# Splitting weights on the side: first parts in two small tiles, second parts in place, and output weights loaded two by two

## The chip, the core and the metric

The kernel runs on one core of a Trainium2 chip, in one launch. Engines named here: TensorE (PE in the profile; PEld is its weight load), VectorE (DVE), ScalarE (ACT), GpSimd (POOL), and SyncE (SP, which here only issues DMAs). The metric is the device time of one launch in microseconds, median of several runs. The kernel before takes 1472.05 us (three runs, 1471.54 to 1473.36).

## The reference

Eight batches of eight attention heads (sequence 576, head dimension 64) go through a landmark attention; the result, 4608 tokens of 512, through two expert layers:

```python
A, Bm, C = sm(q, k_lm), sm(q_lm, k_lm), sm(q_lm, k)      # 32 landmarks
for _ in range(6):
    Z = 2 * Z - Z @ Bm @ Z
x = A @ Z @ C @ v                    # then reshaped to (4608, 512)
x = ((x @ w1) * (x @ w2) @ w3) @ w_out            # d_ff 1024
h = x @ w_in                                      # d_ff 2048
out = where(h > 0, h, exp(min(h, 0)) - 1) @ w_out
```

The weights arrive as float64.

## The kernel before

Matrix products are done in a split form: a float32 value is cut into a first part (`hi`, rounded to the form in which TensorE multiplies) and a second part (`lo`, what is left), and a product takes three matmuls (hi by hi, hi by lo, lo by hi).

Three stages follow each other. In the first, some 117 us, the weights of the first layer are converted from float64 and `w3 @ w_out` is formed. In the second, up to some 690 us, the eight batches run: attention of the next batch, made of small matmuls and many small steps on DVE and ACT, is woven into the matmuls of the first layer (lines 689 to 691, `ab`, and 716 to 718, `y`). A batch has 16 units, a unit has two half steps, and after each half step `fill` (line 874) issues what stands in the tables: steps of the attention of the next batch, loads of `k` (unit 6), `v` (11) and `q` (14) for the batch after the next, and one tick of a `Pipe`. In the third, 690 us to the end, the second layer runs: 72 steps `hh(u)` (42 matmuls, 7 products of half-size blocks, lines 794 to 796, tile `hm`) and `oo(u)` (24 matmuls, lines 849 to 851, tile `o`), two steps apart. `hh(u)` needs the weights `wh` of its step, loaded again for each step into three buffers (`load_wh`, line 738); `oo(u)` needs two of the 16 tiles `wo2`, loaded once (`load_wo`, line 743).

What the change touches is the preparation of these weights in the second stage. `pipe2` holds 32 jobs as Python generators: for each of 8 pairs `p`, two jobs (`wh_first`, `wh_second`) that turn 256 rows of `w_in` into a float32 tile `wx` of seven blocks, and two (`wo_job`) that make a tile of `w_out`. A `yield` ends a job's part of a half step. `join_bits` (line 148) loads the float64 values (SP, line 154), waits two half steps, takes an absolute value on ACT (line 162), four steps on DVE (169 to 172), and two on POOL (174, 176). Then `spill_parts` (line 180) makes both parts on POOL (a cast, line 185, and a subtraction, line 186) in one tile `hl`, and writes it to DRAM by a DMA on SP (line 189): four times for a `wx`, once for a tile of `w_out`. The tile `hl` is there once; a mutex (`hold("hl")`) lets one such piece be under way at a time in program order, and the next cast waits on the chip until the write has read the tile.

Each engine works through its own instructions in the order in which the program issues them, and SP's DMA instructions wait in line too: a load behind a write isn't issued before the write is. POOL also makes the second part `atl` of the attention matrix (line 513), which the matmuls of line 690 need, and issues all loads of `wh` and `wo2` in the third stage.

```python
hl = mlp.tile([128, 2, 512], F32R, name=nm, tag="w2c")
pool.tensor_copy(hl[:, 0, :n], x)
pool.tensor_tensor(hl[:, 1, :n], x, hl[:, 0, :n].bitcast(F32), op=ALU.subtract)
for _ in range(GAP):
    yield
sp.dma_start(out=dst, in_=hl[:, :, :n].bitcast(F32))
held.remove("hl")
```

Of the kernel before, what the change touches and what calls it, by code (L numbers as in the profile page):

```python
# [8 lines left out]
F32 = mybir.dt.float32  # L9
F32R = mybir.dt.float32r  # L10
# [4 lines left out]
ALU = mybir.AluOpType  # L15
# [13 lines left out]
K2 = F2 // 128  # L29
# [7 lines left out]
NPAIR = K2 // 2  # L37
# [9 lines left out]
KS = 15  # L47
QS = 20
RATE = 1.6
GAP = 1  # L50
CONV = (1, 5, 11, 14, 18)
M2 = 5
M3 = 10
# [11 lines left out]
def nystrom_moe_kernel(ctx, tc, qT, kT, vm, vr, w12, w3T, w_out1, w_in2, w_out2, out):  # L65
    nc = tc.nc
    pe, dve, act, pool, sp = nc.tensor, nc.vector, nc.scalar, nc.gpsimd, nc.sync
# [69 lines left out]
            if c.done is not None:  # L137
                c.done()

    held = set()  # L140

    def hold(what):

        while what in held:
            yield
        held.add(what)

    def join_bits(c, ahead=2, ready=lambda: True):

        n = 512
        c.raw = c.p.tile([128, 4 * n + 4], U16, name=f"{c.nm}_raw", tag="raw", bufs=3)
        sp.dma_start(out=c.raw[:, 1 : 1 + 4 * n], in_=c.src.bitcast(U16))
        c.top = c.raw[:, 4 : 4 + 4 * n : 4]
        c.mid = c.raw.bitcast(U32)[:, 1 : 1 + 2 * n : 2]
        for _ in range(ahead):
            yield
        while not ready():
            yield  # L160
        c.y = c.t("y", "cy", BF16)
        act.activation(c.y, c.top.bitcast(BF16), AF.Abs)
        yield
        yield from hold("join")
        c.two, c.tt = c.t("s", "cs", U16, 1), c.t("t", "ct", F32)
        c.lead = c.t("p", "cp", U16)
        act.mul(c.tt, c.mid, 2.0 ** -36)
        yb = c.y.bitcast(U16)
        dve.tensor_scalar(yb, yb, E_MIN, E_MAX, op0=ALU.max, op1=ALU.min)
        dve.tensor_scalar(c.lead, yb, E_MIN, 8.0, op0=ALU.subtract, op1=ALU.mult)  # L170
        dve.scalar_tensor_tensor(c.lead, c.top, 0x8000, c.lead, op0=ALU.bitwise_and, op1=ALU.bitwise_or)
        dve.tensor_scalar(c.two, c.lead, 0xFF80, None, op0=ALU.bitwise_and)
        yield
        pool.tensor_tensor(c.tt, c.tt, c.two.bitcast(BF16), op=ALU.mult)
        c.x = c.x()
        pool.tensor_tensor(c.x, c.tt, c.lead.bitcast(BF16), op=ALU.add)
        held.remove("join")
        yield

    def spill_parts(nm, x, dst):  # L180

        n = x.shape[-1]
        yield from hold("hl")
        hl = mlp.tile([128, 2, 512], F32R, name=nm, tag="w2c")
        pool.tensor_copy(hl[:, 0, :n], x)
        pool.tensor_tensor(hl[:, 1, :n], x, hl[:, 0, :n].bitcast(F32), op=ALU.subtract)
        for _ in range(GAP):
            yield
        sp.dma_start(out=dst, in_=hl[:, :, :n].bitcast(F32))
        held.remove("hl")  # L190

    def wo_job(c, dst):
        yield from join_bits(c)
        yield from spill_parts(f"{c.nm}_hl", c.x, dst)

    wx = {}

# [14 lines left out]
    def wh_second(c, p):  # L212


        c.x = lambda: wx[p][:, 2:4, :].rearrange("p a n -> p (a n)")
        yield from join_bits(c, ready=lambda: p in wx)
        x = wx[p]
        a11, a12, a22, a21, s1, s2, s3 = [x[:, k, :] for k in range(7)]
        pool.tensor_tensor(s1, a21, a22, op=ALU.add)
        pool.tensor_tensor(s3, a11, a21, op=ALU.subtract)  # L220
        yield
        pool.tensor_tensor(s2, s1, a11, op=ALU.subtract)
        pool.tensor_tensor(a21, a12, s2, op=ALU.subtract)
        for k in range(0, 7, 2):
            m = min(2, 7 - k)
            yield
            yield from spill_parts(
                f"wh{p}{k}", x[:, k : k + m, :].rearrange("p a n -> p (a n)"),
                wh_d[p][:, :, k : k + m, :].rearrange("p h a n -> p h (a n)"),
            )  # L230
        held.remove("wx")

    cst = ctx.enter_context(tc.tile_pool(name="cst", bufs=1))
# [6 lines left out]
    wh_d = dram.tile([NPAIR, 128, 2, 7, 2 * 128], F32, name="wh_d")  # L240
# [324 lines left out]
    with tc.manual_schedule():  # L565
# [55 lines left out]
        for o in ORDER:  # L621
            if o == "A":
                k, n_wo = n_wo, n_wo + 1
# [49 lines left out]
        mlp = mlp_ctx.enter_context(tc.tile_pool(name="mlp", bufs=1))  # L673
# [53 lines left out]
        for p in range(NPAIR):  # L727
            pipe2.add(wh_first(Conv(cvp, f"w2{2 * p}", w_in2[2 * p]), p))
            pipe2.add(wh_second(Conv(cvp, f"w2{2 * p + 1}", w_in2[2 * p + 1]), p))
            for f in (2 * p, 2 * p + 1):  # L730
                c = Conv(cvp, f"wo2{f}", w_out2[f * 128 : (f + 1) * 128, :])
                c.x = lambda c=c: c.t("x", "cx", F32)
                pipe2.add(wo_job(c, wo_d[f]))
# [4 lines left out]
        def load_wh(u):  # L738
            t = p2r.tile([128, 2, 7, 256], F32R, name=f"wh{u}", tag="wh", bufs=NWH)
            pool.dma_start(out=t, in_=wh_d[u % NPAIR])  # L740
            wh[u] = t

        def load_wo(p, f):
            t = p.tile([128, 2, DM], F32R, name=f"wo2_{f}")
            pool.dma_start(out=t, in_=wo_d[f])
            wo2[f] = t

        def load_y(i):
            ys[i] = p2r.tile([128, KD, TB], F32, name=f"yin{i}", tag="yin")
            sp.dma_start(out=ys[i], in_=yd[:, :, i * TB : (i + 1) * TB])  # L750
# [4 lines left out]
        def sums_y(i, k):  # L755

            if k == 0:
                tv[i] = [p2r.tile([128, 2, TH], F32, name=f"tv{i}{n}", tag=f"tv{n}") for n in range(4)]
            t1, t2, t3, t4 = tv[i]
            o, a, b = (  # L760
                (t1, block(i, 0, 1), block(i, 0, 0)), (t2, block(i, 1, 1), t1),
                (t3, block(i, 1, 1), block(i, 0, 1)), (t4, block(i, 1, 0), t2),
            )[k]
            pool.tensor_tensor(o, a, b, op=ALU.subtract)

        def parts_y(i, k):

            t1, t2, t3, t4 = tv[i]
            src = (block(i, 0, 0), t2, block(i, 1, 0), t1, t3, block(i, 1, 1), t4)[k]
            hi, lo = [p2r.tile([128, 2, TH], F32R, name=f"yb{w}{i}{k}", tag=f"yb{w}{k}") for w in range(2)]  # L770
            act.copy(hi, src)
            dve.tensor_tensor(lo, src, hi.bitcast(F32), op=ALU.subtract)
            yb[i, k] = (hi, lo)
# [6 lines left out]
        def hh(u):  # L780

            i, _ = units2[u]
            w = wh.pop(u)
            ps = [ps_at.tile([128, 512], F32, name=f"hm{u}", tag="at")]
            ps += [ps_mm.tile([128, 512], F32, name=f"hm{u}{n}", tag="mm") for n in range(2)]
            ps += [ps_at.tile([128, 512], F32, name=f"hm{u}3", tag="at")]
            for k in range(7):
                bank, col = divmod(k + 1, 2)
                o = ps[bank][:, col * TH : (col + 1) * TH]
                bh, bl = yb[i, k]  # L790
                for kk in range(2):
                    cs = slice(kk * 128, (kk + 1) * 128)
                    ah, al = w[:, 0, A_OF[k], cs], w[:, 1, A_OF[k], cs]
                    pe.matmul(o, ah, bh[:, kk, :], start=(kk == 0), stop=False)  # L794
                    pe.matmul(o, ah, bl[:, kk, :], start=False, stop=False)  # L795
                    pe.matmul(o, al, bh[:, kk, :], start=False, stop=(kk == 1))  # L796
            hq[u] = ps
# [6 lines left out]
        def first(u):  # L804
            sq[u] = p2r.tile([128, 1, TH], F32, name=f"s1{u}", tag="s1", bufs=2)
            act.copy(sq[u][:, 0, :], hq[u][0][:, TH:])
# [86 lines left out]
        for u in range(nu + LAG):  # L893
            if u < nu:
                b, n, fc = units[u]
# [34 lines left out]
        p2 = ctx.enter_context(tc.tile_pool(name="p2", bufs=1))  # L930
# [6 lines left out]
        for f in range(4):  # L937
            load_wo(p2, f)
        load_wh(NWH)
        for f in range(4, K2):  # L940
            load_wo(p2, f)
        for u in range(1, n2 + LAG2):
            if u < n2:
                i, p = units2[u]
                if u > 1 and u + NWH - 1 < n2:
                    load_wh(u + NWH - 1)
                hh(u)
                first(u)
                if i + 1 < NBL:
                    if p == 1:  # L950
                        load_y(i + 1)
                    if 3 <= p < 7:
                        sums_y(i + 1, p - 3)
                    if p == NPAIR - 1:
                        for k in range(7):
                            parts_y(i + 1, k)
                combine(u)
                elu(u)
            if u >= LAG2:
                oo(u - LAG2)  # L960
# [51 lines left out]
```

## Time and profile before

| | |
|---|---|
| median of the runs | 1472.05 us |
| the profiled execution | 1470.82 us |
| its span | 1469.0 us |
| PE busy | 1383.8 us (94%) |
| DVE busy | 1084.8 us (74%) |
| ACT busy | 630.7 us (43%) |
| POOL busy | 368.2 us (25%) |
| mean granted TensorE clock | 0.979 of full |

A busy PE is not PE at its peak, and where the granted clock is below 1.00 a matmul takes longer, so time is lost in busy stretches as well. A view of waits says which engine sat idle before which line, and what released it. A release by several semaphores is put down to the one that came last.

### The profile page before, as it was taken

What the parts mean: (1) busy time and instruction counts of PE and PEld (TensorE: products, weight loads), DVE (VectorE), ACT (ScalarE), POOL (GpSimd) and SP (SyncE); (2) the same over time, 40 slices, a digit from 0 to 9 for tenths busy, and PEclk for the clock granted to TensorE, in tenths of its full rate; (3) what the DMA queues carried; (4) which work ended last, traced back from release to release, by engine and by line L of the source; (5) the groups of instructions that cost most, each with busy time, mean ns of one, the idle gap of its engine ahead of it and who ended that gap; (6) DMA issues with size and microseconds to landing.
All of it is one profiled execution on the core that took longest, in us unless ns stands there. A gap on an engine that the chain in (4) does not pass through costs nothing.

```text
span 1469.0 us, 27075 instructions
## 1 busy us (share of the span) xinstructions
PE 1383.8 (94%) x10848; PEld 1187.3 (81%) x10848; DVE 1084.8 (74%) x2003; ACT 630.7 (43%) x1266; POOL 368.2 (25%) x378
## 2 busy tenths in 40 slices
PE   5777999989899998999799999999999999999998
PEld 2335888778778786899789898989898989898987
DVE  7898778668777675653867787878788787877774
ACT  5535443434344444333434444444345353444442
POOL 4442345353545352520310201011010101101000
PEclk9988999999999999999999999999999999999999
DMA  8644243433544434241965556564655555565540
GB/s 305 227 140 147 100 167 138 153 121 128 189 142 162 153 120 157 98 174 51 378 239 202 202 192 217 192 214 166 228 181 212 196 212 197 180 229 179 187 165 29
DMA packets 56653, 259.69 MB, mean 177 GB/s; under 512 B 4816, under 2 KB 15056, under 8 KB 44240
## 3 DMA queue, kind: packets, MB, share of 16 engines
q0 software_dynamic: 12672, 140.51, 26.5%
q1 hardware_dynamic: 43856, 117.45, 22.7%
q8 instruction: 85, 1.39, 0.4%
q14 instruction: 40, 0.33, 0.1%
HBM read 216.01 MB, written 41.94 MB: 176 GB/s over the span
## 4 chain that ended last, share of the span: by engine, by line
PE 73%; DVE 11%; DMA 8%; POOL 4%; issue 2%; ACT 1%; SPq 0%; DVEq 0%; POOLq 0%; ACTq 0%
PE o L851 9%; PE o L850 9%; PE o L849 9%; PE hm L794 8%; PE hm L795 8%; PE hm L796 8%; PE y L716 3%; PE ab L689 3%; PE ab L690 3%; PE ab L691 3%; PE y L717 3%; PE y L718 3%; DMA wh_d<-wh 3%; DMA q<-in_qT_dram 2%; PE m L311 2%
## 5 line engine op out<-in xcount | busy, mean ns | idle before, releaser
L794 PE MATMUL hm<-yb,wh 128*128 128x256 f32 x1008 | 287.4, 285 | 9.9 <-DMA wh<-wh_d 6.3
L795 PE MATMUL hm<-yb,wh 128*128 128x256 f32 x1008 | 286.9, 285 | 0.0
L796 PE MATMUL hm<-yb,wh 128*128 128x256 f32 x1008 | 286.6, 284 | 0.0
L851 PE MATMUL o<-wo,el 128*128 128x512 f32 x576 | 225.6, 392 | 0.0
L850 PE MATMUL o<-wo,eh 128*128 128x512 f32 x576 | 225.3, 391 | 0.0
L849 PE MATMUL o<-wo,eh 128*128 128x512 f32 x576 | 224.0, 389 | 0.0
L825 ACT ACTIVATE t<-m 128x512 f32<-128x512 f32 x144 | 89.9, 624 | 307.0 <-DVE m L823 307.0
L794 PEld LDWEIGHTS hm<-yb,wh 128*128 128x128 f32 x1008 | 194.9, 193 | 13.6 <-issue 6.7
L795 PEld LDWEIGHTS hm<-yb,wh 128*128 128x128 f32 x1008 | 194.8, 193 | 2.8
L796 PEld LDWEIGHTS hm<-yb,wh 128*128 128x128 f32 x1008 | 194.9, 193 | 0.0
L740 POOL DMA_DIRECT2D wh<-wh_d x72 | 39.5, 549 | 616.1 <-PE hm L796 615.8
L716 PE MATMUL y<-gh,w3oh 128*128 128x288 f32 x512 | 161.5, 315 | 2.9 <-DVE w3ol L71 2.9
L689 PE MATMUL ab<-ath,mh 128*128 128x288 f32 x512 | 158.2, 309 | 5.9 <-ACT a L698 3.2
L690 PE MATMUL ab<-atl,mh 128*128 128x288 f32 x512 | 153.2, 299 | 7.2 <-POOL atl L513 7.2
L828 DVE SCALAR_TENSOR_TENSOR t<-m,t 128x512 f32<-128x512 f32 x144 | 99.0, 688 | 78.0 <-ACT m L826 78.0
L691 PE MATMUL ab<-ath,ml 128*128 128x288 f32 x512 | 152.5, 298 | 0.0
L718 PE MATMUL y<-gh,w3ol 128*128 128x288 f32 x512 | 151.7, 296 | 0.0
L717 PE MATMUL y<-gl,w3oh 128*128 128x288 f32 x512 | 151.6, 296 | 0.0
L700 DVE TENSOR_TENSOR g<-ab,a 128x288 f32<-128x288 f32 x128 | 57.7, 451 | 102.0 <-ACT gh L70 52.9
L716 PEld LDWEIGHTS y<-gh,w3oh 128*128 128x128 f32 x512 | 96.8, 189 | 42.3 <-issue 28.9
L851 PEld LDWEIGHTS o<-wo,el 128*128 128x128 f32 x576 | 108.1, 188 | 22.7
L849 PEld LDWEIGHTS o<-wo,eh 128*128 128x128 f32 x576 | 108.5, 188 | 20.9
(146 smaller groups left out, 2786.3 us busy)
## 6 DMA issues: line engine op xcount, KB each, us to landing
wh<-wh_d POOLq DMA_DIRECT2D x72, 1792.0 KB, 7.8
wo_raw<-in_w_out_dram SPq DMA_DIRECT2D x24, 512.0 KB, 5.2
wh_d<-wh SPq DMA_DIRECT2D x24, 512.0 KB, 3.3
k<-in_kT_dram SPq DMA_DIRECT2D x8, 1152.0 KB, 7.2
q<-in_qT_dram SPq DMA_DIRECT2D x8, 1152.0 KB, 6.0
yd<-ysb SPq DMA_DIRECT2D x16, 576.0 KB, 3.6
yin<-yd SPq DMA_DIRECT2D x9, 1024.0 KB, 9.9
out_dram<-osb SPq DMA_DIRECT2D x36, 256.0 KB, 2.3
```

What stands on the lines that cost most here:

```text
L689: pe.matmul(p[:, :NH], mh[:, cs], ah[:, blk, :], start=(blk == 0), stop=False)
L690: pe.matmul(p[:, :NH], mh[:, cs], al[:, blk, :], start=False, stop=False)
L691: pe.matmul(p[:, :NH], ml[:, cs], ah[:, blk, :], start=False, stop=(blk == 1))
L716: pe.matmul(a[oc][:, :NH], w3o_hi[fc][:, os_], gh, start=(fc == 0), stop=False)
L717: pe.matmul(a[oc][:, :NH], w3o_hi[fc][:, os_], gl, start=False, stop=False)
L718: pe.matmul(a[oc][:, :NH], w3o_lo[fc][:, os_], gh, start=False, stop=(fc == K1 - 1))
L794: pe.matmul(o, ah, bh[:, kk, :], start=(kk == 0), stop=False)
L795: pe.matmul(o, ah, bl[:, kk, :], start=False, stop=False)
L796: pe.matmul(o, al, bh[:, kk, :], start=False, stop=(kk == 1))
L849: pe.matmul(a, eh[:, ts_], w[:, 0, :], start=first, stop=False)
L850: pe.matmul(a, eh[:, ts_], w[:, 1, :], start=False, stop=False)
L851: pe.matmul(a, el[:, ts_], w[:, 0, :], start=False, stop=last)
```

## The change

`spill_parts` becomes `first_part`. Only the first part has a tile of its own, of half the size and in two buffers; the second part is written over the float32 values that it is made from (`wx`, or the tile `x` of `w_out`). Two pieces may be under way at a time (`spills`). A first part is written out two half steps after POOL's instructions are issued (`GAP = 2`), and the piece counts as done one half step later. Second parts are written by one DMA per `wx` (all seven blocks) and one per tile of `w_out`; `wx` is free for the next pair one half step after its write is issued. In the third stage four of the output weights' tiles are loaded ahead, and the others two by two in the steps u = 1 to 6, each time ahead of the load of `wh`.

```diff
-GAP = 1
+GAP = 2
...
-    held = set()
+    held, spills = set(), []
...
-    def spill_parts(nm, x, dst):
+    def first_part(nm, x, dst):
 
         n = x.shape[-1]
-        yield from hold("hl")
-        hl = mlp.tile([128, 2, 512], F32R, name=nm, tag="w2c")
-        pool.tensor_copy(hl[:, 0, :n], x)
-        pool.tensor_tensor(hl[:, 1, :n], x, hl[:, 0, :n].bitcast(F32), op=ALU.subtract)
+        while len(spills) > 1:
+            yield
+        spills.append(nm)
+        hi = mlp.tile([128, 512], F32R, name=nm, tag="w2c", bufs=2)
+        pool.tensor_copy(hi[:, :n], x)
+        pool.tensor_tensor(x.bitcast(F32R), x, hi[:, :n].bitcast(F32), op=ALU.subtract)
         for _ in range(GAP):
             yield
-        sp.dma_start(out=dst, in_=hl[:, :, :n].bitcast(F32))
-        held.remove("hl")
+        sp.dma_start(out=dst, in_=hi[:, :n].bitcast(F32))
+        yield
+        spills.remove(nm)
 
     def wo_job(c, dst):
         yield from join_bits(c)
-        yield from spill_parts(f"{c.nm}_hl", c.x, dst)
+        yield from first_part(f"{c.nm}_hi", c.x, dst[:, 0, :])
+        sp.dma_start(out=dst[:, 1, :], in_=c.x)
...
-            yield from spill_parts(
+            yield from first_part(
                 f"wh{p}{k}", x[:, k : k + m, :].rearrange("p a n -> p (a n)"),
-                wh_d[p][:, :, k : k + m, :].rearrange("p h a n -> p h (a n)"),
+                wh_d[p][:, 0, k : k + m, :].rearrange("p a n -> p (a n)"),
             )
+        sp.dma_start(out=wh_d[p][:, 1, :, :], in_=x)
+        yield
         held.remove("wx")
...
-        for f in range(4, K2):
-            load_wo(p2, f)
         for u in range(1, n2 + LAG2):
             if u < n2:
                 i, p = units2[u]
+                if u < NPAIR - 1:
+                    for f in (2 * u + 2, 2 * u + 3):
+                        load_wo(p2, f)
                 if u > 1 and u + NWH - 1 < n2:
                     load_wh(u + NWH - 1)
                 hh(u)
```

Three places in the order of the instructions. First POOL, in the second stage, where the blocks of the second pair (`wx1`; its pieces are `wh12` to `wh16`) and a tile of `w_out` (`wo23`) are cut up, ahead of the second part of the next attention matrix (`atl20`). Before:

```order
L174 TENSOR_TENSOR wo23_t_2694<-wo23_t_2694,wo23_s_2693 128x512
L176 TENSOR_TENSOR wo23_x_2740<-wo23_t_2694,wo23_p_2695 128x512
L185 CAST wh14_2758<-wx1_2250 128x512
L186 TENSOR_TENSOR wh14_2758<-wx1_2250,wh14_2758 128x512
L185 CAST wo23_hl_2785<-wo23_x_2740 128x512
L186 TENSOR_TENSOR wo23_hl_2785<-wo23_x_2740,wo23_hl_2785 128x512
L185 CAST wh16_2861<-wx1_2250 128x256
L186 TENSOR_TENSOR wh16_2861<-wx1_2250,wh16_2861 128x256
L513 TENSOR_TENSOR atl20_2877<-atf_2_2846,ath20_2876 128x576
```

And now:

```order
L174 TENSOR_TENSOR wo23_t_2694<-wo23_t_2694,wo23_s_2693 128x512
L176 TENSOR_TENSOR wo23_x_2743<-wo23_t_2694,wo23_p_2695 128x512
L187 CAST wo23_hi_2761<-wo23_x_2743 128x512
L188 TENSOR_TENSOR wo23_x_2743<-wo23_x_2743,wo23_hi_2761 128x512
L187 CAST wh14_2861<-wx1_2253 128x512
L188 TENSOR_TENSOR wx1_2253<-wx1_2253,wh14_2861 128x512
L519 TENSOR_TENSOR atl20_2878<-atf_2_2846,ath20_2877 128x576
L187 CAST wh16_2966<-wx1_2253 128x256
L188 TENSOR_TENSOR wx1_2253<-wx1_2253,wh16_2966 128x256
```

The subtraction now writes where it reads, and `atl20` stands ahead of the pair's last piece. Second SP, the same place in the program, with the loads of `v3`, `q3` and the next float64 weights (`w24_raw`) among the writes. Before:

```order
L189 DMA wh_d_70<-wh12_2690 256x1x512
L261 DMA v3_2742<-in_vm_dram 128x2048
L262 DMA v3_2742<-in_vr_dram 64x512
L189 DMA wh_d_70<-wh14_2758 256x1x512
L189 DMA wo_d_71<-wo23_hl_2785 128x1024
L189 DMA wh_d_70<-wh16_2861 256x1x256
L265 DMA q3_2922<-in_qT_dram 128x2304
L154 DMA w24_raw_3035<-in_w_in2_dram 128x2048
```

And now:

```order
L191 DMA wh_d_70<-wh12_2738 128x512
L191 DMA wo_d_71<-wo23_hi_2761 128x512
L198 DMA wo_d_71<-wo23_x_2743 128x512
L191 DMA wh_d_70<-wh14_2861 128x512
L271 DMA q3_2923<-in_qT_dram 128x2304
L191 DMA wh_d_70<-wh16_2966 128x256
L235 DMA wh_d_70<-wx1_2253 128x1792
L154 DMA w24_raw_3041<-in_w_in2_dram 128x2048
```

The load of `q3` stands ahead of the write of `wh16`, and the write of all second parts (`wx1`) behind it. Third POOL at the start of the third stage, (`wh3` to `wh7` are the weights of steps 3 to 7; the `tv` make block sums of `y` for the next 512 tokens). Before, from the load of the twelfth output weight on:

```order
L745 DMA wo2_11_8945<-wo_d_71 128x1024
L745 DMA wo2_12_8947<-wo_d_71 128x1024
L745 DMA wo2_13_8949<-wo_d_71 128x1024
L745 DMA wo2_14_8951<-wo_d_71 128x1024
L745 DMA wo2_15_8953<-wo_d_71 128x1024
L740 DMA wh4_9032<-wh_d_70 128x3584
L740 DMA wh5_9137<-wh_d_70 128x3584
```

And now:

```order
L746 DMA wh3_8953<-wh_d_70 128x3584
L751 DMA wo2_4_8955<-wo_d_71 128x1024
L751 DMA wo2_5_8957<-wo_d_71 128x1024
L751 DMA wo2_6_9036<-wo_d_71 128x1024
L751 DMA wo2_7_9038<-wo_d_71 128x1024
L746 DMA wh4_9040<-wh_d_70 128x3584
L751 DMA wo2_8_9145<-wo_d_71 128x1024
L751 DMA wo2_9_9147<-wo_d_71 128x1024
L746 DMA wh5_9149<-wh_d_70 128x3584
```

Before, `wo2_4` to `wo2_15` all stood between `wh3` and `wh4`; now four of them do, and two between `wh4` and `wh5`.

## Rows read from the trace of the kernel before

**Rows 1.** Windows: length, busy time by engine, granted clock, DMA share, GB/s.

```profile
160.00:690.00 530.00, 503.21 (x5291) 433.10 (x5290) 368.63 (x816) 224.99 (x539) 220.81 (x213) 0.98 0.40 141
690.00:746.00 56.00, 46.07 (x292) 42.85 (x292) 33.20 (x54) 17.67 (x33) 14.56 (x24) 0.91 0.84 311
746.00:1469.00 723.00, 719.23 (x4488) 650.73 (x4486) 554.62 (x886) 311.28 (x549) 73.52 (x94) 1.00 0.53 189
```

**Rows 2.** Timeline of PE: start, length, what, in brackets idle time and releaser.

```profile
201.10 1.69 PE L311 MATMUL m<-w_sb,z 64*32 64x512 f32 x16 [1.53 <-DVE ml L473]
573.19 1.68 PE L311 MATMUL m<-w_sb,z 64*32 64x512 f32 x16 [1.21 <-DVE ml L473]
736.69 0.55 PE L794 MATMUL hm<-yb,wh 128*128 128x256 f32 x1 [6.32 <-DMA wh<-wh_d]
```

**Rows 3.** Timeline of POOL, start of the third stage.

```profile
703.07 2.16 POOL L745 DMA_DIRECT2D wo<-wo_d  x4 [43.86 <-ACT t L825]
...
723.84 0.53 POOL L740 DMA_DIRECT2D wh<-wh_d  x1 [0.98 <-PE hm L796]
```

**Rows 4.** DMA issues: what, queue, count, KB each, median us to landing.

```profile
wh<-wh_d POOLq DMA_DIRECT2D x72, 1792.0 KB, 7.8
wh_d<-wh SPq DMA_DIRECT2D x24, 512.0 KB, 3.3
q<-in_qT_dram SPq DMA_DIRECT2D x8, 1152.0 KB, 6.0
...
wh_d<-wh SPq DMA_DIRECT2D x8, 256.0 KB, 2.7
```

**Rows 5.** Windows behind three stalls, and the one from 703 to 736.

```profile
267.00:275.00 8.00, 7.81 (x52) 5.60 (x53) 3.81 (x7) 2.81 (x7) 0.01 (x1) 0.79 0.66 241
...
563.00:570.00 7.00, 6.14 (x38) 4.35 (x39) 0.82 (x2) 1.81 (x4) 0.81 (x1) 0.62 0.85 277
...
736.00:745.00 9.00, 8.31 (x45) 8.21 (x46) 2.29 (x4) 0.37 (x1) 0.22 (x1) 0.64 0.81 324
...
703.00:736.00 33.00, 24.53 (x145) 21.82 (x144) 26.61 (x42) 14.73 (x26) 13.37 (x22) 0.94 1.11 412
```

**Rows 6.** Waits of PE from 160 to 690 us: total, times, longest.

```profile
PE ab L690 <- POOL atl L513: 7.2, 2, 4.3
PE m L311 <- DVE ml L473: 6.3, 4, 1.9
...
PE ab L689 <- ACT a L698: 3.2, 1, 3.2
PE ab L689 <- DVE g L700: 2.7, 1, 2.7
```

**Rows 7.** Chain of waits ahead of two of these stalls: start, length, what.

```profile
264.94 0.73 POOL wh L186
...
266.29 5.59 DMA q<-in_qT_dram
...
316.45 1.60 POOL wo_hl L186
...
318.51 5.52 DMA w_raw<-in_w_in_dram
```

**Rows 8.** Waits of POOL, DVE and SP's queue, whole span.

```profile
POOL wo_hl L185 <- DMA wh_d<-wh: 38.3, 12, 5.2
...
POOL wh L185 <- DMA wo_d<-wo_hl: 23.4, 9, 3.7
POOL wh L185 <- DMA wh_d<-wh: 22.9, 9, 3.5
...
DVE qsum L296 <- DMA q<-in_qT_dram: 9.3, 5, 2.5
```

**Rows 9.** The longest waits of SP's queue.

```profile
SPq L189 <- POOL wh L186: 163.0, 30, 17.4
...
SPq L189 <- POOL wo_hl L186: 90.3, 16, 8.0
```

## The prediction

> **What bounds the kernel now.** I read the windows by stage first, then who PE waits for, then the chain of waits ahead of those stalls. From 746 us on PE is busy all the time at a granted clock of 1.00 [rows 1]; nothing that the change does there can show. The first stage has the same instructions as before. What is left is 160 to 690 us, where PE is idle for 530 − 503.2 = 26.8 us and the mean clock is 0.98, and 690 to 746 us, where it is idle for 9.9 us at 0.91 [rows 1].
>
> In the second stage four kinds of wait are to be seen: for `atl` from POOL (7.2 us, two times), for `ml` from DVE (6.3, four times), for `a` from ACT (3.2) and for `g` from DVE (2.7) [rows 6], together 19.4 us. The chain shows one source behind them. POOL ends a piece of the splitting at 264.94 + 0.73 = 265.67, SP issues its write, and only then, at 266.29, the load of `q` that stood behind it; POOL at 316.45 + 1.60 = 318.05 lets go of a write, and the float64 weights behind it leave at 318.51 and land at 324.03 [rows 7]. DVE then sits at its `q` sums (9.3 us, five times [rows 8]), and ACT at its absolute value, each with work for PE behind it in its queue. POOL is late because each cast waits until the one tile `hl` has been written out: 38.3 + 23.4 + 22.9 = 84.6 us over 30 waits [rows 8]. SP's queue waits 163.0 + 90.3 = 253.3 us over 46 writes, 5.5 us each [rows 9].
>
> A stall of some 2 us or more is followed by the lower of TensorE's two clocks (1.2 in place of 2.4 GHz) for a while: over the 8 us from 267 the granted clock is 0.79, which costs 8 × 0.21 = 1.7 us; the stalls for `a`, for `g` and the longest for `ml` show the same 1.7. After the longest for `atl` it is 0.62 over 7 us [rows 5], 2.7 us, some 2.2 when the idle time in that window is left out. That makes 4 × 1.7 + 2.2 = 9.0 us. In the third stage step 4 (`hm`) starts at 736.69 after 6.32 us of waiting for its weights [rows 2], and the 9 us from 736 run at 0.64 [rows 5]: 3.2 us, some 3.0 without the idle part.
>
> **The change part by part.**
>
> *Output weights two by two.* The load of the weights for step 4 is issued at 723.84, behind 12 loads of `wo2` [rows 3], and lands when PE has waited from 730.4 on. In the window 703 to 736 the DMAs move 412 GB/s [rows 5], so bytes decide. Now eight tiles (4.2 MB) and `wh3` (1.8 MB) stand ahead of it, with its own 1.8 MB 7.9 MB in all (the size of `wh` from [rows 4]; a tile of `wo2` is 128 x 1024 float32); from 703.07 [rows 3] at 412 GB/s that lands at 703.1 + 19.1 = 722.2 by estimate, 8 us ahead of 730.4. Step 5 comes one step later (723 us [rows 1] over 68 steps of 66 matmuls, 10.6 us), and two more tiles and its weights, 2.9 MB, take 7.0 us. From then on the same 2.9 MB fall on 10.6 us, 273 GB/s, well under 412. The loads of `wo2` now wait behind a load of `wh` that waits for a buffer; the tiles of step u + 2 are asked for in step u, and used in `oo` two steps later or more. So the wait goes and its clock with it: 6.3 + 3.0 = 9.3 us. Bounds: 6.3 if the slow clock came anyway, 9.3 if not. I take 9.3, because nothing else stands still there.
>
> *Two tiles for first parts.* The 84.6 us of POOL's waits become short ones: a buffer comes round after two pieces, and the next piece is let in one half step after the write was issued. A half step is (573.19 − 201.10) / 5 / 32 = 2.3 us (the same instruction five batches apart [rows 2]), a write of 256 KB lands in 2.7 [rows 4]. So POOL waits at most some 0.4 us behind SP. Together with `atl` moving ahead of the pair's last piece this lets `atl` run earlier by the waits of the four or so pieces in a row ahead of it, 84.6 / 30 = 2.8 us each, some 11 us where 4.3 were missing.
>
> *Writes two half steps later.* SP comes to each write 2.3 us later, and POOL is done 84.6 / 46 = 1.8 us earlier on average, more at the end of a row of pieces, where `q` stands. Of 5.5 us per write 4.1 go on average. The loads behind need little: `q` was missed by 9.3 / 5 = 1.9 us [rows 8], the float64 weights by 3.2 [rows 6]. I take both as covered.
>
> *Second parts in place.* The same number of POOL instructions of the same shapes; the trace shows no subtraction that writes over its input. From nothing to twice the 0.73 us of the nearest row [rows 7], 35 us over 48 pieces, it would stay in POOL's idle time, since POOL is busy for 221 of 530 us [rows 1]; I take nothing. There are 24 more writes, 0.6 us of SP each by the 265.67 to 266.29 of [rows 7], 15 us of a queue that waited 253.
>
> *An added wait.* The next pair's first write to `wx` (POOL, line 176) now waits for the 896 KB write. Queued behind it is POOL's splitting, `atl` at times, and PE waits for that. By interpolation between 3.3 us for 512 KB and 6.0 for 1152 KB [rows 4] it lands in 4.9 us; a pair comes to that instruction no sooner than three half steps after the issue, 7.0 us. Cost between nothing and 7 times 4.9 = 34 us of POOL; I take nothing.
>
> **Sum.** 19.4 + 9.0 + 9.3 = 37.7 us if all goes and nothing comes. Other waits of PE (26.8 − 19.4 = 7.4 us) stay. Jobs shift by some half steps against the attention's steps, so ACT and DVE meet them in other places: one load of `k` now stands behind more pieces than before. I give 5 us back for new stalls, two of the size of those above with their clock. 1470.8 (the profiled execution, 1.8 of it outside the span) − 32.7 = 1438.1; the median of the runs is 1.2 above that execution: **1439 us**.
>
> **Rivals.**
>
> *SP stays the bound.* 4.1 of 5.5 us is an average; if SP still blocks `q` and the float64 weights, the change doesn't do what its delay says. Then the two stalls for `atl` go with their clock (7.2 + 1.7 + 2.2 = 11.1) and the 9.3: 1472 − 20 = 1452. For it: single waits of SP reach 17.4 us [rows 9]. Against: those long ones end with POOL's work, not with a write.
>
> *Only the third stage.* New stalls of the moved jobs eat the second stage's gain: 1472 − 9 = 1463. Against: DVE waits at five of the six loads of `q` in this stage, and where it doesn't, no stall for `ml` follows.
>
> *POOL bound by its writes: slower.* If POOL waits out every write (48 first parts at 2.7 us = 130, and 34 for `wx`: 164 us in place of 84.6), then by today's ratio of 28.4 us lost on PE for 84.6 waited the second stage loses 55 in place of 28.4; less 9.3, the time is 1472 + 17 = 1489. It decides from some 112 us of POOL waiting on, where 28.4 + 9.3 us are used up. Against it is the half step between issue and reuse. The Trainium skill has a rule in this direction ("DMA: Bandwidth & Descriptors", Anatomy of one DMA): a transfer costs about 2.0 us fixed plus its bytes at 436 GB/s, so many small ones pay more. The trace agrees on the price (by the rule 2.6 and 3.2 us, 2.7 and 3.3 measured); by the rule the 24 added writes would cost 24 × 2.0 = 48 us if each stood in the path.
>
> **How the numbers follow.** Forecast 0.65, SP stays the bound 0.16, only the third stage 0.10, slower 0.05, and 0.04 for no change in sum. The range goes from 1430, which is the full 37.7 us and some 4 of the other 7.4 us of waits, to 1462, which takes in the second case and most of the third. A measurement of this kernel can tell about 0.2%, 3 us, from no change: faster 0.91, same 0.04, slower 0.05.
>
> **What would show it.** Right: step 4 without a wait for `wh`, the clock at 1.00 from 735 on; POOL's waits for `wh_d` and `wo_d` under 20 us; no wait of DVE at `q`; PE idle in the second stage under 12 us. Wrong: waits for `atl` or `ml` still there; POOL waiting at line 176 for `wx`; SP's writes still waiting for POOL some 5 us each.

## The result and the profile after

The changed kernel takes 1436.34 us (four runs, 1435.87 to 1437.29) beside 1471.8 us before: a ratio of 0.976 with a 95% interval of 0.9743 to 0.9777, 35.5 us or 2.4% faster. The forecast was 1439. The profiled execution has a span of 1434.4 us at a mean clock of 0.989.

The windows by stage answer to [rows 1]. After the time range and its length stand the busy times of PE, PEld, DVE, ACT and POOL, then the granted clock, the DMA share and GB/s:

```profile
160.00:660.00 500.00, 487.79 (x5252) 422.87 (x5253) 370.86 (x811) 223.03 (x533) 220.91 (x213) 1.00 0.43 149
660.00:690.00 30.00, 26.39 (x202) 25.45 (x201) 15.26 (x28) 11.24 (x23) 6.40 (x12) 1.00 0.51 183
690.00:746.00 56.00, 56.00 (x347) 50.51 (x346) 47.09 (x76) 25.36 (x45) 11.55 (x16) 1.00 0.88 331
```

In the second stage PE was idle for 26.8 of 530 us; now it is for 12.2 of 500, and the mean clock is 1.00 to two places, where it was 0.98. The third stage begins with step 0, whose first matmul is in the timeline of PE, before and after:

```profile
690.09 0.28 PE L794 MATMUL hm<-yb,wh 128*128 128x256 f32 x1
```

```profile
665.63 0.28 PE L800 MATMUL hm<-yb,wh 128*128 128x256 f32 x1
```

So of the 34.6 us by which the span fell, 24.5 lie ahead of the third stage, and the rest in it: 1469.0 − 690.1 = 778.9 us before, 1434.4 − 665.6 = 768.8 after, 10.1 us.

PE's waits in the second stage, in answer to [rows 6] (total, times, longest):

```profile
PE n L418 <- DVE X L408: 4.5, 4, 1.7
PE m L317 <- DVE at L488: 3.4, 3, 2.2
PE ct L429 <- ACT e L338: 2.8, 3, 1.3
PE ab L695 <- ACT a L704: 0.9, 1, 0.9
PE m L317 <- DVE ml L479: 0.7, 1, 0.7
```

None is left for `atl` and for `g`; those for `a` and `ml` fell from 9.5 to 1.6 us. Two others grew: for `at` from 0.7 to 3.4 us, for `e` from 0.9 to 2.8. POOL waits for a write once in the whole span, in answer to [rows 8], and no line has DVE waiting for `q`:

```profile
POOL wh L187 <- DMA wh_d<-wh: 1.3, 1, 1.3
```

But SP's queue still stands at these writes, in answer to [rows 9]:

```profile
SPq L191 <- POOL wh L187: 108.9, 22, 16.1
...
SPq L191 <- POOL wo_hi L187: 55.7, 16, 6.3
```

That is 164.6 us over 38 writes, 4.3 us each, and yet the loads behind them come in time.

At the start of the third stage POOL's timeline, in answer to [rows 3], shows the weights of step 4 issued 684.57 − 678.65 = 5.9 us behind the first `wo2`, where it was 20.8 before:

```profile
678.65 2.16 POOL L751 DMA_DIRECT2D wo<-wo_d  x4 [43.77 <-ACT t L831]
680.78 0.56 POOL L746 DMA_DIRECT2D wh<-wh_d  x1
681.30 2.16 POOL L751 DMA_DIRECT2D wo<-wo_d  x4
684.57 0.53 POOL L746 DMA_DIRECT2D wh<-wh_d  x1 [1.11 <-DMA wo<-wo_d]
```

### The profile page after: what moved, and what is told of

Its sections match the earlier page's. It is cut to its first block, busy times and chain, and to the rows that moved or that the text cites. A ratio compares the mean times of both kernels' runs of the same rounds, so it can differ in the third digit from the quotient of the medians.

```text
span 1434.4 us, 27127 instructions
## 1 busy us (share of the span) xinstructions
PE 1370.2 (96%) x10848; PEld 1179.0 (82%) x10848; DVE 1088.0 (76%) x2003; ACT 630.8 (44%) x1266; POOL 368.3 (26%) x378
## 4 chain that ended last, share of the span: by engine, by line
PE 83%; DVE 13%; ACT 1%; issue 1%; DMA 1%; SPq 0%; DVEq 0%; ACTq 0%
PE o L857 9%; PE o L856 9%; PE o L855 9%; PE hm L800 8%; PE hm L801 8%; PE hm L802 8%; PE y L722 5%; PE ab L695 4%; PE ab L696 4%; PE ab L697 4%; PE y L724 4%; PE y L723 4%; PE m L317 2%; DVE w_b L128 1%; DVE w_b L124 1%
## 5 line engine op out<-in xcount | busy, mean ns | idle before, releaser
L800 PEld LDWEIGHTS hm<-yb,wh 128*128 128x128 f32 x1008 | 192.9, 191 | 6.9 <-ACT s L812 4.0
L801 PEld LDWEIGHTS hm<-yb,wh 128*128 128x128 f32 x1008 | 192.9, 191 | 2.8
L802 PEld LDWEIGHTS hm<-yb,wh 128*128 128x128 f32 x1008 | 193.0, 192 | 0.0
L855 PEld LDWEIGHTS o<-wo,eh 128*128 128x128 f32 x576 | 108.5, 188 | 20.9
L856 PEld LDWEIGHTS o<-wo,eh 128*128 128x128 f32 x576 | 108.1, 188 | 21.2
```

The lines of the kernel that those rows point to most:

```text
L855: pe.matmul(a, eh[:, ts_], w[:, 0, :], start=first, stop=False)
L856: pe.matmul(a, eh[:, ts_], w[:, 1, :], start=False, stop=False)
```

## The experiments

Ten kernels, timed against the kernel before, which measured 1471.0 to 1471.9 us in their rounds; each ratio is to the kernel before of the same round. "Second stage ends" is the start of step 0 in the profiled execution, "third" the rest of the span.

| kernel | median us | ratio, 95% | second stage ends | third |
|---|---|---|---|---|
| before | 1471.8 | | 690.1 | 778.9 |
| changed | 1436.3 | 0.9743 to 0.9777 | 665.6 | 768.8 |
| e1_gap2 | 1448.3 | 0.9822 to 0.9855 | 669.4 | 777.9 |
| e2_loads | 1464.0 | 0.9935 to 0.9964 | 691.8 | 770.8 |
| e3_all_gap1 | 1436.6 | 0.9749 to 0.9777 | 666.3 | 770.0 |
| e4_all_early | 1446.2 | 0.9814 to 0.9843 | 665.2 | 778.8 |
| f1_two_tiles_same_order | 1432.0 | 0.9706 to 0.9740 | 661.2 | 768.5 |
| f2_one_tile_same_order | 1433.4 | 0.9714 to 0.9744 | 662.6 | 769.9 |
| g1_spaced | 1445.1 | 0.9801 to 0.9834 | 664.0 | 779.6 |
| h1_early_s | 1434.8 | 0.9730 to 0.9760 | 666.6 | 767.7 |
| j1_slow_casts | 1459.7 | 0.9894 to 0.9947 | 688.6 | 770.0 |
| i1_combined | 1427.8 | 0.9674 to 0.9722 | 659.7 | 766.3 |

**The parts.** First the delay alone (on the kernel before), the loads alone (on the kernel before), and each taken out of the changed kernel.

```diff
-GAP = 1
+GAP = 2
```

> Kernel before, only GAP = 2 (writes issued two half steps after POOL's work; one tile hl with both parts). Theory A, POOL's waits on the one tile are the source: they stay at some 85 us, the two stalls for atl stay, only part of the q and float64 loads come earlier; 1462 to 1472 us. Theory B, SP's line is the source: DVE's waits at q and the stalls for a and g go with their clock (6.3 + 3.2 + 2.7 + 6.8 = 19 us), 1453 us.

1448.3 us: theory B's direction, by more than it said. What B didn't foresee is how. POOL's waits on its one tile are all still there, 39.6 + 24.0 + 17.3 + 9.1 = 90.0 us by the view of POOL's waits of this kernel:

```profile
POOL wh L185 <- DMA wh_d<-wh: 39.6, 10, 6.8
POOL wh L185 <- DMA wo_d<-wo_hl: 24.0, 9, 4.3
POOL wo_hl L185 <- DMA wh_d<-wh: 17.3, 7, 3.5
POOL wo_hl L185 <- DMA wo_d<-wo_hl: 9.1, 2, 5.3
```

And SP stands at the writes as before (154.3 and 73.8 us over 43 writes, 5.3 each). Yet no wait for `atl` is left. The order of the program tells why: a mutex that is held half a step longer pushes the next piece back, and so two pieces of the pair in the first excerpts of the order ahead of the prediction now stand behind `atl20` and behind the load of `q3`.

```diff
         load_wh(NWH)
-        for f in range(4, K2):
-            load_wo(p2, f)
...
+                if u < NPAIR - 1:
+                    for f in (2 * u + 2, 2 * u + 3):
+                        load_wo(p2, f)
                 if u > 1 and u + NWH - 1 < n2:
```

> Kernel before, only the output weights loaded two by two. Step 4 doesn't wait for wh, the clock stays at 1.00; the third stage is 10.1 us shorter as in the changed kernel (778.9 to 768.8), the second stage the same: 1461.7 us. Rival: part of those 10 us came from a second stage that ended otherwise; then 1463 to 1466.

1464.0, 7.1 us less (5.3 to 9.6 by the interval): inside the rival's range. The wait for `wh` is gone, but the third stage takes 770.8 us, 2 more than in the changed kernel. The clock is the reason. In every kernel up to here PE waits 2.77 us at step 2 of this stage, and over the 6 us behind that wait the granted clock is 0.72 before, 1.00 in the changed kernel and 0.50 in e2:

```profile
707.31:713.31 6.00, 5.92 (x35) 5.72 (x36) 4.71 (x9) 2.42 (x4) 2.15 (x5) 0.72 1.10 416
682.86:688.86 6.00, 5.92 (x45) 5.63 (x46) 4.71 (x9) 2.42 (x4) 2.19 (x5) 1.00 1.07 399
709.03:715.03 6.00, 6.00 (x28) 6.00 (x29) 4.71 (x9) 2.41 (x4) 2.22 (x5) 0.50 1.08 407
```

That is 1.7 us lost before, none in the changed kernel and 3.0 here, in a place that no edit so far touches. So 1.7 of the 10.1 us by which the changed kernel's third stage is shorter don't come from the loads.

On the changed kernel, the delay taken out:

```diff
-GAP = 2
+GAP = 1
```

> Changed kernel with GAP = 1. Theory A: POOL's waits stay away (under 10 us for writes), so most of the second stage's 24.5 us stay: 1437 to 1443 us. Theory B: SP comes to each write 2.3 us earlier and stands longer in front of q and the float64 weights; DVE waits at q again for 5 us or more, some 12 to 19 us are lost: 1448 to 1455.

1436.6, the same as with `GAP = 2`. So the delay is worth nothing in time once the tiles are two; theory A's side. It does move the loads: the first `q` is issued at 184.8 us with it and at 191.6 without. DVE then waits at `q` for 2.0 us, three times, and no stall of PE for `q`'s sums follows. SP waits 104.4 + 78.2 = 182.6 us over 42 writes here, the same 4.3 each as with the delay.

And the loads put back ahead of the steps (the lines of e2's edit, the other way round):

> Changed kernel with the 12 output weights loaded in one go again. The wait for wh of some 6.3 us and the low clock behind it come back in the third stage, the second stage stays as in the changed kernel: 1446 us. If the parts are not independent, less than 7 us come back.

1446.2, as expected: 9.9 us come back, in the third stage alone (778.8), with a wait of 7.0 us for `wh`. What is left, 24.8 us below the kernel before of that round, and e2's 7.1 make 31.9, 3.6 short of the whole; by the granted clocks some 2.7 of that is lost behind step 2 (1.3 more in e2 than before, 1.4 more in e4 than in the changed kernel).

So either the delay or the two tiles does nearly the whole work of the second stage. The next runs ask what they have in common.

**Order, waits, and lateness.** The old mutex on the changed kernel puts POOL's instructions back in their old order, with two tiles (f1) and with one (f2):

```diff
-GAP = 2
+GAP = 1
...
-        while len(spills) > 1:
-            yield
-        spills.append(nm)
+        yield from hold("hl")
...
-        yield
-        spills.remove(nm)
+        held.remove("hl")
```

```diff
-        hi = mlp.tile([128, 512], F32R, name=nm, tag="w2c", bufs=2)
+        hi = mlp.tile([128, 512], F32R, name=nm, tag="w2c", bufs=1)
```

> Changed kernel with GAP = 1 and the old mutex (one piece at a time, let go when its write is issued): POOL's instructions of the second stage stand in exactly the order of the kernel before; two tiles for first parts and second parts in place stay, output weights two by two. Theory P, POOL's waits on its tile are the source: they go, and with them the stalls for atl, a, g and ml; 1436 to 1441 us. Theory O, the places of the pieces ahead of atl and of the load of q are the source: the stalls stay; 1459 to 1464 us (the 1464.0 with the loads two by two alone).

1432.0: theory P's direction, and below its range. POOL waits 0.8 us for a write in all, and PE's idle time in the second stage is the least of all kernels so far:

```profile
PE n L415 <- DVE X L405: 5.8, 3, 2.5
PE ct L426 <- ACT e L335: 0.9, 1, 0.9
PE m L314 <- DVE at L485: 0.4, 2, 0.2
```

> As f1_two_tiles_same_order, with one tile for first parts instead of two: only the number of tiles differs. Theory P: POOL waits for each write again, some 2 us or more for a write of 256 KB, 60 to 85 us in all, and the stalls come back in most places: 1455 to 1464 us. Theory O: no difference from f1. If in-place second parts and smaller writes are what helped: 1437 to 1441 as well.

1433.4: theory P fails here. The third expectation has the reason, smaller writes with second parts in place, though the time is 4 us below its range. Beside f1 the intervals overlap, so the second tile buys nothing that is clear of the noise. With one tile POOL waits for its writes, but for 34 us and not for 84.6:

```profile
POOL wo_hi L185 <- DMA wh_d<-wh: 17.1, 11, 3.5
POOL wh L185 <- DMA wh_d<-wh: 9.7, 5, 4.6
POOL wh L185 <- DMA wo_d<-wo_hi: 7.2, 7, 2.9
```

A write of a first part alone, 256 KB, lands in 2.1 us by the median, one of both parts took 3.3 [rows 4]. That some waits may stay without a stall says that there is a margin, and that the stalls come where it is used up.

The mutex of the kernel before, held half a step longer without the delay:

```diff
         sp.dma_start(out=dst, in_=hl[:, :, :n].bitcast(F32))
+        yield
         held.remove("hl")
```

> Kernel before, GAP = 1, but the mutex is let go one half step after the write is issued: POOL's order is the same as with GAP = 2 alone (two pieces behind atl and q), each write is issued one half step after POOL's work as before. If GAP = 2 alone gained by spacing the pieces: 1446 to 1450 us, as that one (1448.3), POOL's waits unchanged or smaller. If it gained by SP coming to the writes later: 1463 to 1471.

1445.1, somewhat below the delay alone (1448.3), with intervals that overlap: what `GAP = 2` gained on the kernel before, the spacing of the pieces gives by itself. No part of SP coming later to the writes is to be seen.

That leaves the theory that a row of pieces must not end later than some point, whatever makes it late. The test puts the lateness back without the waits: one tile, small writes, the old order, and each cast done three times.

```diff
-        pool.tensor_copy(hi[:, :n], x)
+        for _ in range(3):
+            pool.tensor_copy(hi[:, :n], x)
```

> As f2_one_tile_same_order (one tile, the old order, small writes, second parts in place), with each cast done three times: some 1.2 us more of POOL per piece, 48 pieces. Lateness theory (the stalls come when a row of four to six pieces ends a few us late, whatever makes it late): 5 to 7 us more per row brings DVE's wait at q, the stalls for atl, a and g back in most places: 1445 to 1462 us. Theory that the smaller writes themselves did it (traffic, write landing): 1433 to 1437 us, no such stalls.

1459.7 us, inside the range of the lateness theory. POOL waits for writes less than in f2 (13.1 + 6.7 + 5.1 = 24.9 us), and the stalls are back: PE waits for `atl`, `a`, `g` and `ml`, and the second stage ends at 688.6 us, 26.0 behind f2. The added casts lengthen DVE's work too, 383.4 us busy in this stage beside 374.4 in f2; but g1 has 380.0 and no such stalls, so that alone isn't the cause.

```profile
PE m L315 <- DVE ml L477: 5.3, 3, 2.5
...
PE ab L694 <- POOL atl L517: 3.3, 2, 2.8
...
PE ab L693 <- ACT a L702: 2.0, 2, 1.4
```

The margin can be read at the loads of `q` (least, median and most time of the issue, then the start of the first and the last of six). The first one stands behind the same pieces in the kernel before, in f2 and in j1, which these lines show in that order:

```profile
L265 SPq DMA_DIRECT2D q<-in_qT_dram x6: 328/559/561, 192.2 to 563.1; - x6
```

```profile
L268 SPq DMA_DIRECT2D q<-in_qT_dram x6: 337/382/392, 188.0 to 536.2; - x6
```

```profile
L269 SPq DMA_DIRECT2D q<-in_qT_dram x6: 328/384/803, 193.8 to 559.7; - x6
```

It takes some 6 us to land. Before, DVE has waited for the first of them when its sum starts at 198.17:

```profile
198.17 0.75 DVE L296 TENSOR_REDUCE qsum<-q 128x32 f32<-128x576 f32 x1 [1.62 <-DMA q<-in_qT_dram]
```

Issued at 188.0 it is there in time; at 192.2 it is late by that wait, at 193.8 by 0.3 us, and DVE waits at five of six loads, 9.3 and 8.5 us in all. The float64 weights show the same, and by more. ACT's waits for them before, in f2, and in j1:

```profile
ACT w_y L162 <- DMA w_raw<-in_w_in_dram: 22.3, 5, 8.0
ACT w_y L162 <- DMA w_raw<-in_w_in_dram: 5.2, 4, 2.0
ACT w_y L162 <- DMA w_raw<-in_w_in_dram: 20.0, 5, 7.1
```

Before, the two longest of them, 8.0 and 7.0 us, end at 324.05 and 387.39, and PE's stalls for `a` and `g` end behind them, at 325.59 and 392.71. In the changed kernel ACT waits 2.2 us in all. A few microseconds of POOL decide over some 25 of PE.

**A faster version.** The wait of 2.77 us at step 2 of the third stage, in every kernel so far, is for a copy on ACT that stands behind step 0's elu. h1, made from the changed kernel, puts that copy ahead (`elu_end` is the second half of `elu`, in the kernel before from line 827 on):

```diff
-        elu(0)
...
                 first(u)
+                if u == 1:
+                    elu(0)
...
                 combine(u)
+                if u == 1:
+                    elu_end(0)
                 elu(u)
+                elu_end(u)
```

> Changed kernel, with the copy s of step 1 on ACT ahead of step 0's elu, and the combination of step 1 on DVE ahead of the second half of step 0's elu: the wait of step 2 in the third stage (2.77 us for ACT s) and the low clock behind it (1.7 us) go: 1432 us. Rival: oo(0) waits for the later elu of step 0 instead: 1435 to 1438.

1434.8, at the edge of the rival's range, but not by its reason. The low clock that the expectation counted on saving is not in the changed kernel, where the clock behind that wait is 1.00. The wait for the copy is gone, and step 3, now earlier, waits for its weights, which stood behind four `wo2`:

```profile
693.69 0.36 PE L800 MATMUL hm<-yb,wh 128*128 128x256 f32 x1 [2.06 <-DMA wh<-wh_d]
```

The last kernel takes f1's second stage, h1's edit, and loads these weights behind two `wo2` instead of four:

```diff
-        for f in range(4):
+        for f in range(2):
             load_wo(p2, f)
         load_wh(NWH)
+        for f in range(2, 4):
+            load_wo(p2, f)
```

> f1_two_tiles_same_order (old order, GAP = 1, two tiles) with the third stage's start as in h1_early_s and the weights of step 3 loaded ahead of the third and fourth output weight. Second stage as f1 (ends at 661 us), step 2 and step 3 of the third stage without a wait, no low clock: 1432.0 - 4.5 = 1427.5 us. Rival: step 3's weights or the later elu hold PE up for 2 us or more again: 1430 to 1432.

1427.8 us, 8.6 us below the changed kernel by the medians. The number is as expected, in part by luck: 4.5 us were to come from the third stage, a low clock of 1.7 among them that f1 doesn't have behind its wait. Step 3 waits 0.52 us, and the third stage takes 766.3, 2.2 less than in f1; the second stage, with f1's instructions, ended 1.5 us earlier in the profiled execution.

## Why the prediction was right, and where it wasn't

*The output weights*: the term was 9.3 us, the profile shows 10.1, and taking it out again brought back 9.9 (e4). The mechanism, bytes ahead of one load, was the one predicted. Alone on the kernel before it measured 7.1 (e2), with an interval that just reaches the term. The close fit is partly luck: 1.7 of the 10.1 us are the clock behind step 2's wait, which was lower before and not in the changed kernel. With the clock behind that wait set equal (0.76 over 6 us in e4), the third stages of the changed kernel, e2 and e4 give 8.4, 9.4 and 8.6 us by estimate.

*The second stage*: 28.4 us were counted and 5 given back, 23.4; the profile shows 24.5, of which 14.6 are idle time of PE and 9.9 busy time at a lower clock, where 9.0 were counted for the clock. The gain is made as the chain said, at waits for `q`, for float64 weights and for `atl`, all in line behind pieces of the splitting, and the clock that followed them. The 5 us given back for moved jobs are there too: f1, with the old order, has 7.1 us of idle time in the second stage and ends it at 661.2, the changed kernel has 12.2 and ends at 665.6. Their size was a guess that came out by luck: two stalls with their clock were taken, and what came are 4.6 us more of waits for `at` and `e`, with no low clock over the 8 us behind the longest of them. So the sign "PE idle under 12 us" was just missed.

*Two tiles for first parts*: POOL's waits fell from 84.6 to 1.3 us, where under 20 were forecast. The prediction took these waits for the source. They were one way of being late: f2 keeps 34 us of them and e1 90, without the stalls, and j1 has the stalls with 24.9. Smaller writes with second parts in place are enough (f2), and so are pieces further back (e1 and g1). Two tiles alone, with writes of both parts, were not run. Which of these is at work in the changed kernel cannot be said.

*Writes two half steps later*: this step failed. "Of 5.5 us per write 4.1 go on average" measured 5.5 to 4.3, 1.2 us, and the delay as such is worth nothing: with two tiles the time is the same without it, and so are SP's 4.3 us (e3), and with one tile its gain is that of the spacing (g1). A mean over all writes said nothing on the few that stand ahead of `q`. By the same error the rival that SP stays the bound was put at 1452: SP does stay at its writes, and the loads come in time all the same. Nor were the float64 weights missed by 3.2 us: that row is PE's wait for `a`, while ACT waited for these loads up to 8.0 us, more than the 4.1 counted. e3, without the delay, has ACT's waits for them at 0.2 us, so they don't need this step.

*Second parts in place* and *the added wait*: nothing, as taken. POOL is busy for 220.9 us of the second stage, where it was 220.8, and no wait at the first write to `wx` (line 176) is in the trace. But "nothing" hid a gain: smaller first writes, which second parts in place allow, are a cure without the second tile (f2), which the prediction didn't see, because it took the two tiles and the smaller writes for one edit.

*POOL bound by its writes*: this rival fell, with 1.3 us of waits where it decides from 112. The median of a first part's write of 256 KB is 2.1 us, in f2 as in the changed kernel. The rule of the Trainium skill that the prediction weighed there ("DMA: Bandwidth & Descriptors", Anatomy of one DMA: a fixed cost for each transfer) gives 2.6 us; the Trainium skill states it there for transfers that GpSimd issues, and these are issued by SP. No run shows a cost of the 24 added writes: f1 has them, and the least idle time of PE up to there.

*The clock*: the prediction let a stall of some 2 us or more be followed by the lower clock. The five stalls of the second stage that it priced were, but it doesn't hold each time: in the changed kernel and in f1 the clock stayed at 1.00 behind waits of 2.2 to 2.8 us.

## What to carry to other kernels

Where an engine's waits come from side work that stands ahead in an in-order queue, look for the few instructions that are needed soon, and by how many microseconds they miss; the total of the waits in that queue says little. Several edits that each clear a small margin don't add up, so try the one that moves nothing else first: here smaller writes in the old order were worth 3 (one tile) to 4 us (two tiles) more than the change with all its parts. Loads that are needed one by one go out in the order of need.

## What the runs showed of the hardware beyond that

Waits of the same length don't always cost the same clock. Behind the same wait of 2.77 us, with the same instructions, the granted clock over 6 us was 1.00 in the changed kernel and 0.50 in e2 (the lines stand beside e2), and the first matmul took 0.58 us in e1, e2, e3 and e4, and 0.39 in the changed kernel, f1, f2, g1 and j1. In the second stage the same wait of 2.17 us for `at` was followed by 1.00 over 8 us in the changed kernel and by 0.79 in e3:

```profile
395.70:403.70 8.00, 7.07 (x55) 5.60 (x56) 7.72 (x13) 3.64 (x9) 5.88 (x6) 1.00 0.01 2
328.25:336.25 8.00, 8.00 (x54) 6.10 (x55) 5.31 (x11) 3.08 (x8) 1.42 (x1) 0.79 0.04 14
```

So idle time alone doesn't order two kernels: e3 has 9.5 us of it in the second stage and ends it at 666.3, the changed kernel has 12.2 and ends at 665.6. What decides over the clock no run here shows.

With the old `elu`, the third stage took 768.5 to 770.8 us with loads two by two and 777.9 to 779.6 with early loads.
